# A fused attention, routing and feed-forward kernel: its pieces up to run 1 in a new sequence, the weights behind run 1's rows, half the rope table, the values' high parts on ScalarE

## The chip, the cores and the metric

One core of one Trainium2 chip runs the whole program. The metric is the device time of one execution in microseconds (us). The kernel before takes 654.41 us, the median of 3 runs (654.29 to 654.86).

## The reference

Three layers, one behind the other, all in float32:

```
q_rot, k_rot = rotate(q), rotate(k)                 # rope; 2 batches, 8 heads, 576 tokens, head size 64
attn = softmax(q_rot @ k_rot.T / 8)                 # per head
x = (attn @ v), heads side by side                  # 1152 tokens x 512
logits = x @ w_gate + log1p(exp(x @ w_noise)) * noise    # 8 experts
top2 experts per token, weights by softmax over the two
out[t] = sum over its two experts e: weight * relu(x[t] @ w1[e]) @ w2[e]      # 512 -> 1024 -> 512
h = out @ w_in;  g = max(h, 0) + log1p(exp(-|h|));  result = g @ w_out        # 512 -> 2048 -> 512
```

## The kernel before, in words

Matmuls of full precision are done as three products of a high and a low part (`mm3`). A value x is split by a copy into the shorter matmul format (the high part, on ScalarE) and a subtraction x - high (the low part, mostly on VectorE).

**Attention.** The 16 heads are worked on in 8 pairs. For each pair SyncE loads q, k and v (`load_pair`, `load_v`), GpSimd applies the rope in pieces (`ro`, `rope`) and splits the values into high and low parts in two passes (`vsplit`, L404 and L405). TensorE transposes q and k (`prep`), ScalarE and VectorE take high and low parts (`ph`, `pl`). Then two DMAs per pair rearrange them inside SBUF: `dq` (`move_queries`, L450) moves the queries to the other half of the partitions, and `dk` (`keys_twice`, L454) copies the keys into the half that the queries left, so `dk` can only be issued when `dq` has landed. Only then can the scores of the pair begin. The scores come in 72 blocks of 128 query rows, 9 per pair: S0 to S8 are pair 0, S9 is the first of pair 1, S13 the first of pair 1 that needs both heads, S36 the first of pair 4, S63 the first of pair 7. Each block n goes through S (TensorE, L479), M (row maximum, VectorE, L492), E (exponential, ScalarE, L501), T (transposes, TensorE, L510), Th and Tl (high and low parts, ScalarE L542 and VectorE L546), A (times the values, TensorE), Ao (copy, ScalarE), X (times the gate weights, TensorE L579), Xd (VectorE, which also issues the store of the rows to the table `xtab` from SyncE, L610 and L612).

**Routing.** The gate logits are added up (`l`). The first four token tiles are routed early (`R`), the others after the last head (`m`), with the ranking of the experts (`k`). That gives the row numbers of run 0 (`ga0` gathers them) and of run 1 (`ga1`, L1019, two indirect DMAs issued by GpSimd).

**Expert runs.** Runs 0 to 8 each take one expert's rows through w1, relu, w2. Run 0's first product (`G`) stands at the end of the planned part. Runs 0 and 1 use the same expert, whose 8 weight chunks of 512 KB are loaded (`ld`, `load_chunk`, L155) and split (`sp` on ScalarE L184, `sl` on VectorE or GpSimd L188) in the planned part. Chunks 8 onwards are loaded by SyncE, four ahead, as soon as the order of the experts is known. The feed-forward layer's weights are decoded and split in between.

**What sets the order.** Everything up to the end of run 0's first product is a list of about 900 pieces, the text `ORDER`, which was worked out offline from a table of pieces with an engine, a cost in ns and predecessors (the calls of `op`). The kernel emits the pieces in this order, so that each engine's queue and SyncE's DMA queue hold their pieces in the order of the list. An engine does not step past an instruction that waits, nor does SyncE's queue.

Of the kernel before, what the change touches and what calls it, by code (L numbers as in the profile page):

```python
# [50 lines left out]
ORDER = """
c0 rf-1 in0 rf0 rf4 rf1 kd0 prep0,2,0 rf5 in1 ph0,2,0 prep0,0,1 pl0,2,0 ph0,0,1 rf2 prep0,0,0 pl0,0,1 ph0,0,0 ro1,0
pl0,0,0 prep0,2,1 ph0,2,1 ro1,1 pl0,2,1 rf3 S0 ro1,2 S1 ro1,3 M0 kd1 lp2 M1 prep0,1,0 E0 ro1,4 prep0,1,1 ph0,1,0 S2
ro1,5 E1 pl0,1,0 ro1,6 ph0,1,1 M2 prep1,2 T0,1 ph1,2 ro1,7 pl0,1,1 S3 E2 pl1,2 ro1,8 prep1,0 Th0,1 M3 S4 ro1,9 ph1,0
Tl0,1 E3 ro1,10 pl1,0 T0,2 T0,0 rope1 M4 Th0,2 dq1,0 S5 Th0,0 vs0 Tl0,2 prep1,1 E4 M5 T0,3 S6 Tl0,0 Th0,3 dk1,0 E5 M6
T0,4 Th0,4 Tl0,3 rs0 S7 T0,5 E6 ro2,0 Tl0,4 Th0,5 lv2 S8 M7 ph1,1 T1,1 ro2,1 M8 A0,0 lp3 E7 Tl0,5 Th1,1 pl1,1 S9 E8
ro2,2 T1,2 Tl1,1 Ao0,0 A0,1 dq1,1 M9 Th1,2 ro2,3 ri0 E9 Tl1,2 T1,0 S10 Ao0,1 Th1,0 T1,4 ro2,4 dk1,1 M10 X0 Th1,4 Tl1,0
E10 S11 Tl1,4 rope2 T1,3 M11 S12 Th1,3 T2,1 Xd0 rs1 E11 lp4 prep2,0 vs1 M12 A1,0 ph2,0 ri1 Tl1,3 Th2,1 pl2,0 S13 Ao1,0
Tl2,1 E12 prep2,2 prep2,1 M13 ph2,2 lv3 T2,0 ph2,1 ro3,0 pl2,2 S14 Th2,0 pl2,1 A1,1 E13 M14 dq2 rs2 Tl2,0 T2,4 Ao1,1
S15 Th2,4 ro3,1 T2,5 M15 X1 E14 Tl2,4 dk2 Th2,5 ro3,2 Xd1 E15 T2,2 Tl2,5 S16 Th2,2 ro3,3 S17 Tl2,2 T2,3 M16 T3,0 Th2,3  # L60
A2,0 ro3,4 E16 Tl2,3 M17 Th3,0 T3,2 Ao2,0 rope3 Tl3,0 A2,1 Th3,2 ri2 E17 Tl3,2 S18 vs2 Ao2,1 prep3,2 T3,4 M18 ph3,2
S19 Th3,4 pl3,2 T3,3 M19 X2 E18 Tl3,4 E19 c1 S20 Xd2 Th3,3 T3,1 M20 S21 Th3,1 Tl3,3 prep3,1 E20 prep3,0 Tl3,1 ph3,1
T4,1 M21 rs3 S22 ph3,0 c3 ro4,0 lv4 pl3,1 E21 pl3,0 T4,0 Th4,1 A3,0 M22 Th4,0 dq3 l1 ro4,1 Tl4,1 E22 S23 Tl4,0 T4,3
M23 S24 ro4,2 Th4,3 T4,2 E23 Tl4,3 dk3 A3,1 Th4,2 l2 M24 rs4 Ao3,0 Tl4,2 T4,4 Ao3,1 S25 ro4,3 Th4,4 X3 M25 E24 Tl4,4
T4,5 ro4,4 E25 lp5 S26 c2 T5,1 ri3 Th4,5 M26 A4,0 Th5,1 rope4 Tl4,5 E26 Xd3 S27 Ao4,0 ri4 rs5 Tl5,1 T5,4 lp6 S28 vs3
Th5,4 ri5 prep4,0 M27 A4,1 ph4,0 M28 E27 Tl5,4 T5,2 Ao4,1 S29 pl4,0 Th5,2 T5,0 E28 M29 X4 Th5,0 Tl5,2 E29 prep4,1 Xd4
S30 ph4,1 Tl5,0 prep4,2 T6,2 ph4,2 ro5,0 pl4,1 S31 Th6,2 pl4,2 M30 dq4 T5,3 M31 l3 A5,0 E30 ro5,1 Tl6,2 Th5,3 S32 E31
Tl5,3 ro5,2 T6,3 Ao5,0 M32 dk4 S33 Th6,3 T6,1 E32 M33 ro5,3 A5,1 Th6,1 Tl6,3 E33 Tl6,1 S34 Ao5,1 ro5,4 T6,0 M34 T6,4
Th6,0 S35 Th6,4 Tl6,0 X5 rope5 M35 E34 T7,1 Tl6,4 E35 rs6 S36 lp7 prep5,2 Th7,1 Xd5 T7,0 l4 ph5,2 Tl7,1 vs4 prep5,0
S37 pl5,2 ph5,0 M36 T6,5 Th7,0 A6,0 M37 E36 pl5,0 Th6,5 S38 l5 Tl7,0 E37 prep5,1 Tl6,5 T7,4 Ao6,0 ro6,0 S39 M38 Th7,4  # L70
T7,2 M39 A6,1 E38 Tl7,4 ro6,1 Th7,2 S40 ph5,1 Tl7,2 E39 pl5,1 ro6,2 T7,3 M40 T8,1 dq5 Th7,3 S41 ri6 Ao6,1 rs7 Tl7,3
A7,0 Th8,1 ro6,3 E40 Tl8,1 T8,2 ri7 M41 T8,0 rs8 Th8,2 dk5 A7,1 Th8,0 Tl8,2 ro6,4 E41 Tl8,0 S42 Ao7,1 T8,4 Ao7,0 M42
S43 rope6 Th8,4 T8,5 ri8 M43 X6 E42 lv6 Tl8,4 E43 S44 Xd6 lv5 Th8,5 prep6,0 M44 X7 ph6,0 Tl8,5 E44 pl6,0 S45 rs9 Xd7
T9,4 T9,1 Th9,4 M45 z1 S46 vs5 ri9 prep6,2 Th9,1 A8,0 Tl9,4 ph6,2 E45 Tl9,1 T8,3 M46 S47 Th8,3 pl6,2 T9,0 E46 M47
prep6,1 Th9,0 Tl8,3 S48 ro7,0 E47 Tl9,0 T9,3 ph6,1 M48 S49 Th9,3 l6 pl6,1 E48 l7 T9,2 Tl9,3 dq6 R0 S50 M49 Ao8,0 R1
T10,2 Th9,2 M50 A8,1 E49 Tl9,2 ro7,1 E50 R2 S51 dk6 Th10,2 S52 ro7,2 Ao8,1 A9,0 M52 R3 T10,0 Tl10,2 Ao9,0 A9,1 Th10,0
ro7,3 M51 Tl10,0 lv7 E51 RP4 T10,5 RF4 T10,4 Ao9,1 ro7,4 S53 Th10,5 X8 Th10,4 Tl10,5 rope7 M53 E52 T10,1 X9 Tl10,4 E53
R6 Th10,1 Xd8 T11,4 S54 Xd9 Th11,4 z2 R7 prep7,2 Tl10,1 S55 ph7,2 prep7,1 Tl11,4 T10,3 ph7,1 pl7,2 cr0 T11,0 Th10,3
M54 A10,0 Th11,0 pl7,1 E54 Tl10,3 prep7,0 Ao10,0 Tl11,0 S56 R8 ph7,0 ld0 T11,2 M55 T11,3 Th11,2 M56 A10,1 Th11,3 ld3
Tl11,2 E55 Tl11,3 R9 T11,1 E56 pl7,0 S57 Th11,1 T12,1 dq7 Ao10,1 S58 Tl11,1 Th12,1 M57 sp0 rs10 T12,2 Tl12,1 A11,0  # L80
Th12,2 l9 M58 E57 vs6 dk7 Tl12,2 T12,0 E58 S59 ri10 Th12,0 T12,3 M59 S60 Ao11,0 Th12,3 Tl12,0 A11,1 E59 M60 sl0 Tl12,3
T12,4 E60 z0 S61 T13,0 Th12,4 M61 S62 rs11 X10 E61 Tl12,4 rs12 Ao11,1 M62 S63 R10 Th13,0 T13,1 E62 M63 A12,0 ld1
Tl13,0 Th13,1 E63 Tl13,1 S64 ld2 Ao12,0 ri11 T13,4 Xd10 T12,5 Th13,4 M64 S65 l10 Th12,5 X11 z3 Tl13,4 rs13 E64 vs7
Tl12,5 T13,3 sp1 M65 S66 T14,0 Th13,3 Xd11 A12,1 E65 ri12 Tl13,3 M66 S67 z4 Th14,0 E66 Tl14,0 T13,2 Ao12,1 M67 RP11
T14,3 Th13,2 RF11 S68 E67 Tl13,2 A13,0 Th14,3 M68 rs14 sp2 Tl14,3 T14,2 ld4 l11 sl1 S69 ga0 Th14,2 T14,1 E68 A13,1
Tl14,2 Ao13,0 Th14,1 M69 T14,4 Ao13,1 S70 Tl14,1 Th14,4 gl0 X12 M70 E69 Tl14,4 T14,5 E70 S71 Xd12 T15,0 Th14,5 M71 l12
X13 Th15,0 ri13 Tl14,5 E71 A14,0 Tl15,0 sp3 Xd13 T15,1 sl2 l13 Ao14,0 T15,4 rs15 Th15,1 A14,1 Th15,4 Tl15,1 ld6 XT1
Tl15,4 Ao14,1 T15,3 XTh1 XT0 XTl1 ld5 T15,2 ri14 XTh0 A15,0 Th15,3 XTl0 Th15,2 Tl15,3 X14 Ao15,0 Tl15,2 sp4 sl3 A15,1
Xd14 ld7 Ao15,1 ri15 l14 sl4 sp5 X15 G0 Xl15 l15 Xd15 m0 G1 m1 Gh0 Gl0 G2 m2 Gh1 m3 Gh2 mP4 Gl2 G3 mF4 Gl1 m6 G4 k0
Gh3 m7 Gl3 G5 Gh4 k1 Gl4 m8 G6 Gh5 k2 sp6 m9 G7 Gh6 sl5 Gl5 mP10 mF10 Gh7 Gl6 ga1 sl6 sp7 k3 sl7 k4 Gl7 k5  # L90
# [1605 lines left out]
```

## Time and profile before

| | |
|---|---|
| time, median of 3 | 654.41 us |
| time of the profiled execution | 653.66 us |
| its span in the profile | 651.8 us |
| TensorE busy | 626.5 us (96%) |
| VectorE busy | 481.3 us (74%) |
| ScalarE busy | 420.3 us (64%) |
| GpSimd busy | 223.4 us (34%) |
| DMA traffic | 109.79 MB |

The page slices the span into 40 equal parts; TensorE's line of tenths there reads 9 nearly everywhere, and the clock line reads 9 except in the first slice. A busy TensorE is not one at its peak, because the ends of its matmuls are modelled; an engine's waits stand in brackets behind its rows in a timeline. The attention ends near 174 us, run 0's first product near 187 us, run 1 begins near 202 us and the feed-forward layer near 437 us.

### The profile page before, as it was taken

Reading aid. Unit: us, or ns where it says so; the run is one execution under the profiler, and the core shown is the slowest. Engines: PE = TensorE matmul, PEld = TensorE weight load, DVE = VectorE, ACT = ScalarE, POOL = GpSimd, SP = SyncE. Lnnn points to the kernel's source line nnn. Section 1 sums busy time; section 2 is a strip of 40 time slices with the busy share of each in tenths; the row PEclk is TensorE's granted clock in tenths of the full one; section 3 lists DMA queues with packets and bytes.
Section 4 is the critical chain, followed back from the end, with each engine's and each line's share of the span. In section 5 each row is a group of like instructions: output and inputs, shape, how many; then the busy total and the mean of one; then the engine's idle time right before and its main releaser. Section 6 shows DMA issues by size and latency. Waiting matters only on the chain.

```text
span 651.8 us, 11560 instructions
## 1 busy us (share of the span) xinstructions
PE 626.5 (96%) x3944; PEld 561.3 (86%) x3944; DVE 481.3 (74%) x979; ACT 420.3 (64%) x883; POOL 223.4 (34%) x318
## 2 busy tenths in 40 slices
...
GB/s 142 118 158 109 168 119 192 167 216 272 114 112 241 220 226 332 311 274 349 303 333 292 342 312 304 278 205 167 126 33 33 33 17 1 48 2 2 33 1 33
DMA packets 70061, 109.79 MB, mean 168 GB/s; under 512 B 11728, under 2 KB 39120, under 8 KB 69616
## 3 DMA queue, kind: packets, MB, share of 16 engines
...
q10 hardware_dynamic: 3426, 5.79, 2.4%
...
HBM read 76.70 MB, written 23.59 MB: 154 GB/s over the span
## 4 chain that ended last, share of the span: by engine, by line
PE 75%; DMA 9%; DVE 6%; issue 4%; ACT 3%; POOL 2%; SPq 0%; DVEq 0%; POOLq 0%; ACTq 0%
PE p L264 9%; PE p L266 9%; PE p L265 9%; PE po L266 5%; PE ph L264 5%; PE ph L265 5%; PE ph L266 5%; PE po L264 5%; PE po L265 5%; PE ps L479 4%; DMA wb<-wb 3%; PE pt L510 3%; PE pa L557 2%; PE p L1282 2%; DMA qT<-wb 1%
## 5 line engine op out<-in xcount | busy, mean ns | idle before, releaser
L233 POOL TENSOR_TENSOR dm<-dm,da 128x512 int32<-128x512 int32 x32 | 41.9, 1310 | 134.4 <-DVE da L230 78.3
L1574 ACT ACTIVATE fa<-ph 128x256 f32<-128x256 f32 (+1 forms) x64 | 26.0, 407 | 69.2 <-PE ph L266 69.2
L492 DVE TENSOR_REDUCE nmx<-ps 128x1 f32<-128x576 f32 x72 | 53.5, 749 | 11.6 <-PE ps L479 11.2
L1264 DVE SCALAR_TENSOR_TENSOR hb<-p,hb 128x256 fp32r<-128x256 f32 (+1 forms) x104 | 31.8, 345 | 33.0 <-ACT hb L1262 32.9
L501 ACT ACTIVATE P<-ps,nmx 128x576 f32<-128x576 f32 x72 | 53.4, 745 | 4.2 <-DVE nmx L492 2.8
L188 DVE TENSOR_TENSOR w<-wraw,w 128x1024 fp32r<-128x1024 f32 x41 | 55.2, 1354 | 0.5 <-ACT w L184 0.5
L1581 DVE TENSOR_SCALAR fu<-fa 128x256 f32<-128x256 f32 (+1 forms) x64 | 19.8, 310 | 46.9 <-ACT fa L1575 46.8
...
L546 DVE TENSOR_TENSOR ptl<-pt,pth 128x512 fp32r<-128x512 f32 x72 | 48.3, 682 | 3.1 <-ACT pth L542 2.4
L542 ACT ACTIVATE pth<-pt 128x512 fp32r<-128x512 f32 x72 | 42.7, 601 | 10.1 <-PE pt L510 9.7
L184 ACT ACTIVATE w<-wraw 128x1024 fp32r<-128x1024 f32 x42 | 44.1, 1055 | 7.1 <-DMA wraw<-in_moe_w_dram 5.6
L264 PE MATMUL p<-xh,w 128*128 128x256 f32 (+3 forms) x152 | 46.5, 306 | 0.0
L265 PE MATMUL p<-xl,w 128*128 128x256 f32 (+3 forms) x152 | 46.5, 306 | 0.0
L266 PE MATMUL p<-xh,w 128*128 128x256 f32 (+3 forms) x152 | 46.5, 306 | 0.0
L188 DVE TENSOR_TENSOR wb<-wraw,wb 128x1024 fp32r<-128x1024 f32 x33 | 45.1, 1374 | 0.2 <-ACT wb L184 0.2
L510 PE MATMUL pt<-ident,P 128*128 128x128 f32 x288 | 43.7, 278 | 1.1 <-DVE ptl L546 0.5
L510 PEld LDWEIGHTS pt<-ident,P 128*128 128x128 f32 x288 | 34.2, 142 | 2.8 <-DVE ptl L546 1.1
L1582 DVE TENSOR_TENSOR fa<-fa,fu 128x256 f32<-128x256 f32 (+1 forms) x64 | 29.4, 460 | 9.6 <-ACT fl L1576 7.4
L184 ACT ACTIVATE wb<-wraw 128x1024 fp32r<-128x1024 f32 x33 | 34.6, 1054 | 0.3 <-DMA wraw<-in_moe_w_dram 0.2
L1262 ACT ACTIVATE hb<-p 128x320 fp32r<-128x320 f32 (+3 forms) x64 | 26.1, 420 | 13.3 <-PE p L266 12.2
L479 PE MATMUL ps<-wb,qT 128*128 128x288 f32 (+1 forms) x160 | 29.6, 314 | 4.8 <-DMA wb<-wb 3.5
L1593 ACT ACTIVATE gh<-fl 128x256 fp32r<-128x256 f32 (+1 forms) x64 | 27.7, 432 | 9.4 <-DVE fl L1587 9.4
...
## 6 DMA issues: line engine op xcount, KB each, us to landing
...
```

The lines of the kernel that those rows point to most:

```text
L184: nc.scalar.activation(hi, r, AF.Copy)
L188: lo_eng.tensor_tensor(out=lo, in0=r, in1=hi.bitcast(F32), op=OP.subtract)
L233: nc.gpsimd.tensor_tensor(out=m, in0=m, in1=ai, op=OP.add)
L264: nc.tensor.matmul(ps, ah, bh, start=first and i == 0, stop=False)
L265: nc.tensor.matmul(ps, ah, bl, start=False, stop=False)
L266: nc.tensor.matmul(ps, al, bh, start=False, stop=last and i == n - 1)
L479: nc.tensor.matmul(ps[:m, a, :HN], QT[p][:, c0:c0 + m], KK[p][:, x, hh, k0:k0 + HN], start=x == 0, stop=x == 1)
L492: nc.vector.tensor_reduce(out=nmx, in_=stS[n][:, :, :HN], axis=AX.XY, op=OP.max, negate=True)
L501: nc.scalar.activation(P_of(n).rearrange("p (a c) -> p a c", a=2), ps[:, :, :HN], AF.Exp, bias=nmx, scale=1.0, accum_out=acc)
L510: nc.tensor.transpose(ps[:, kb, :], Pt[:, kb * 128:(kb + 1) * 128], ident)
L542: nc.scalar.activation(dh, x, AF.Copy)
L546: nc.vector.tensor_tensor(out=dl, in0=x, in1=dh.bitcast(F32), op=OP.subtract)
```

## The change

- `ORDER` is a new list, worked out again from new costs. SyncE's costs are larger (loads of q and k 2150 to 2700 ns, of v 1100 to 2900), some others smaller.
- The store of a head pair's rows is a piece of its own (`xo`) and no longer a part of `Xd`. The loads of the gate weights are a piece of their own (`gt`) and no longer behind `lp2`.
- The high parts of the values move from GpSimd to ScalarE (`vh`); the low parts stay on GpSimd (`vs`).
- The rope table has 5 blocks for each partition instead of 9. It is loaded by SyncE behind the first keys; the other four are copied by ScalarE.
- A DMA of 64 bytes, `seen`, reads run 1's second tile of rows. It stands on SyncE's queue ahead of the loads of chunks 8 to 11.
- The ranking of the experts moves from GpSimd to VectorE except for its last part; 4 of the 10 one-hot rows of the late routing move from VectorE to GpSimd (`oa`).
- The loads of chunks 4 to 7 become pieces of the list (`ld4` to `ld7`); before, the low part of the chunk four earlier issued them.

```diff
 ORDER = """
-c0 rf-1 in0 rf0 rf4 rf1 kd0 prep0,2,0 rf5 in1 ph0,2,0 prep0,0,1 pl0,2,0 ph0,0,1 rf2 prep0,0,0 pl0,0,1 ph0,0,0 ro1,0
+c0 rf-1 in0 rf0 rf4 rf1 kd0 prep0,2,0 rf5 prep0,0,0 ph0,2,0 rf2 ph0,0,0 pl0,2,0 pl0,0,0 prep0,2,1 ph0,2,1 rf3
...
-    def load_pair(p, heads=((0, 2),), queues=(nc.sync, nc.sync)):
+    def load_pair(p, heads=((0, 2),), queues=(nc.sync, nc.sync), then=None):
...
+                if then and i:
+                    then()
...
-    def vsplit(p, eng):
...
-        eng.tensor_tensor(out=tt[:, :, 0:D], in0=xx, in1=zb, op=OP.add)
-        eng.tensor_tensor(out=tt[:, :, D:2 * D], in0=xx, in1=tt[:, :, 0:D].bitcast(F32), op=OP.subtract)
+    def v_hi(p):
+        x, t = v_parts(p)
+        nc.scalar.activation(t[:, :, 0:D], x, AF.Copy)
+
+    def v_lo(p):
+        x, t = v_parts(p)
+        nc.gpsimd.tensor_tensor(out=t[:, :, D:2 * D], in0=x, in1=t[:, :, 0:D].bitcast(F32), op=OP.subtract)
...
+    def X_store(g):
+        b, h = divmod(g, H)
         if h % 2:
...
     def ranks():
...
-        fold(g, above, rank)
-        yield
+        V.tensor_tensor(out=above, in0=kc[:, None, :].to_broadcast(sq), in1=kc[:, :, None].to_broadcast(sq), op=OP.is_lt)
+        V.tensor_reduce(out=rank, in_=above, axis=AX.X, op=OP.add)
...
-        g.tensor_tensor(out=srt[:, 0], in0=ohR, in1=kc[:, None, :].to_broadcast(sq), op=OP.mult)
-        g.tensor_tensor(out=srt[:, 1], in0=ohR, in1=iota8[:, None, :].to_broadcast(sq), op=OP.mult)
-        fold(g, srt, srt[:, :, :, 2])
...
+        V.tensor_tensor(out=srt[:, 0], in0=ohR, in1=kc[:, None, :].to_broadcast(sq), op=OP.mult)
+        V.tensor_tensor(out=srt[:, 1], in0=ohR, in1=iota8[:, None, :].to_broadcast(sq), op=OP.mult)
+        V.tensor_reduce(out=srt2, in_=srt, axis=AX.X, op=OP.add)
...
-    nc.scalar.dma_start(out=cs[:, 0:5], in_=cs_t[:, 0:5])
-    load_pair(0, ((0, 1),), (nc.scalar, nc.sync))
+    load_pair(0, ((0, 1),), (nc.scalar, nc.sync), lambda: nc.sync.dma_start(out=cs[:, 0:5], in_=cs_t))
     nc.scalar.activation(csq[:, 0:5], cs[:, 0:5], AF.Copy, scale=0.125)
-    nc.sync.dma_start(out=cs[:, 5:9], in_=cs_t[:, 5:9])
-    nc.scalar.activation(csq[:, 5:9], cs[:, 5:9], AF.Copy, scale=0.125)
+    nc.scalar.activation(cs[:, 5:9], cs[:, 0:4], AF.Copy)
+    nc.scalar.activation(csq[:, 5:9], cs[:, 0:4], AF.Copy, scale=0.125)
...
-        op(("vs", p), "POOL", 2850, [("A", 2 * p - x, a) for x in (4, 3) for a in (0, 1)] + [("lv", p)] if p > 1 else [("in", 1)], vs_op, p)
+        op(("vh", p), "ACT", 610, [("A", 2 * p - x, a) for x in (4, 3) for a in (0, 1)] + [("lv", p)] if p > 1 else [("in", 1)], v_hi, p)
+        op(("vs", p), "POOL", 1600, [("vh", p)], v_lo, p)
         if p > 1:
-            op(("lv", p), "SP", 1100, [("vs", p - 2)], load_v, p)
+            op(("lv", p), "SP", 2900, [("vs", p - 2)], load_v, p)
         if p > 2:
-            op(("lp", p), "SP", 2150, [("rope", p - 2)], load_pair, p)
+            op(("lp", p), "SP", 2700, [("rope", p - 2)], load_pair, p)
...
-    op(("lp", 2), "SP", 2150, [("rf", 3), ("rf", 5)], lambda: (load_pair(2), load_gates()))
+    op(("lp", 2), "SP", 2700, [("rf", 3), ("rf", 5)], load_pair, 2)
+    op(("gt", 0), "SP", 5600, [], load_gates)
...
+    op(("oa", 0), "DVE", 1440, [("m", 6)], one_hots, nc.vector, 0, 6)
+    op(("oa", 1), "POOL", 2360, [("m", 6)], one_hots, nc.gpsimd, 6, 10)
...
     nxt["order"] = True
+    nc.sync.dma_start(out=seen, in_=XG[1, 1][0:1, 0:16])
     while nxt["load"] < nxt["split"] + 4:
         load_chunk()
...
-    tok = np.stack(four + [512 + p % 64] + four, axis=1)
+    tok = np.stack(four + [512 + p % 64], axis=1)
```

SyncE's queue before, from the first copies of pair 1 (`qT`, `wb`: L450 is `dq`, L454 is `dk`) to the second ones; L366 and L369 load values, L358 and L361 load k and q:

```order
L450 DMA qT_302<-wb_78 64x640 x2
L454 DMA wb_78<-wb_78 64x2x640
L366 DMA w3_140<-in_v_dram 128x2x256
L369 DMA w3_140<-in_v_dram 64x2x64 x2
L358 DMA w3_140<-in_k_dram 128x2x256
L361 DMA w3_140<-in_k_dram 128x1x64
L358 DMA w3_140<-in_q_dram 128x2x256
L361 DMA w3_140<-in_q_dram 128x1x64
L450 DMA qT_302<-wb_78 64x512 x2
L454 DMA wb_78<-wb_78 64x2x640
```

The same place now (L461 is `dq`, L465 is `dk`, L363 and L368 load k and q):

```order
L461 DMA qT_301<-wb_79 64x640 x2
L465 DMA wb_79<-wb_79 64x2x640
L461 DMA qT_301<-wb_79 64x512 x2
L363 DMA w3_141<-in_k_dram 128x2x256
L368 DMA w3_141<-in_k_dram 128x1x64
L363 DMA w3_141<-in_q_dram 128x2x256
L368 DMA w3_141<-in_q_dram 128x1x64
L465 DMA wb_79<-wb_79 64x2x640
```

The second head's queries are no longer queued behind seven loads, and the load of values has left this stretch; the load of k and q stands between the second pair of copies.

SyncE's queue before at the copies of pair 7, with two weight chunks (L155, which need the expert's number from L130):

```order
L1004 DMA ytab_62<-wb_78 128x4x512
L130 TENSOR_LOAD ordA_91
L130 ISA x2
L155 ISA
L155 DMA wraw_1925<-in_moe_w1_dram 128x4x256
L155 ISA
L155 DMA wraw_1963<-in_moe_w1_dram 128x4x256
L450 DMA qT_1852<-wb_78 64x1152 x2
L454 DMA wb_78<-wb_78 64x2560
```

The same place now:

```order
L1016 DMA ytab_62<-wb_79 128x4x512
L461 DMA qT_1834<-wb_79 64x1152 x2
L134 TENSOR_LOAD ordA_92
L134 ISA x2
L159 ISA
L159 DMA wraw_2040<-in_moe_w1_dram 128x4x256
L465 DMA wb_79<-wb_79 64x2560
```

The queries' move now stands ahead of the expert's number and of any weight chunk; one chunk instead of none lies between the move and the keys' copy.

SyncE's queue before at the end of the planned part, from the last chunk of run 0's expert:

```order
L155 DMA wraw_2508<-in_moe_w2_dram 128x2x512
L610 DMA xtab_60<-xs_2520 128x4x128
L612 DMA xtab_60<-xs_2520 64x128
L130 TENSOR_LOAD ordr_92
L130 ISA x2
L155 ISA
L155 DMA wraw_2786<-in_moe_w1_dram 128x4x256
```

The same place now:

```order
L624 DMA xtab_60<-xs_2524 128x4x128
L626 DMA xtab_60<-xs_2524 64x128
L159 ISA
L159 DMA wraw_2573<-in_moe_w2_dram 128x2x512
L1312 DMA seen_63<-yg_2436 1x16
L134 TENSOR_LOAD ordr_93
L134 ISA x2
L159 ISA
L159 DMA wraw_2785<-in_moe_w1_dram 128x4x256
```

The small read of run 1's rows (`seen`) stands ahead of the load of the experts' order and of chunk 8.

## Rows read from the trace of the kernel before

**Rows 1.** PE's timeline: start us, us, operation, count, idle before and releaser.

```profile
30.88 0.37 PE L479 MATMUL ps<-wb,qT 128*128 128x288 f32 x1 [1.36 <-ACT o L568]
...
40.44 1.29 PE L479 MATMUL ps<-wb,qT 128*128 128x288 f32 x8 [0.93 <-DMA wb<-wb]
...
87.03 0.76 PE L479 MATMUL ps<-wb,yg 128*128 128x288 f32 x4 [0.84 <-DMA wb<-wb]
...
144.67 0.77 PE L479 MATMUL ps<-wb,qT 128*128 128x288 f32 x4 [2.54 <-DMA wb<-wb]
...
174.11 1.35 PE L579 MATMUL pa<-Wx,o 128*128 128x96 f32 x10 [0.56 <-ACT o L568]
...
195.11 0.63 PE L1246 MATMUL pa<-ident,yg 128*128 128x128 f32 x4 [0.78 <-DMA yg<-xtab,idx]
...
199.70 0.84 PE L1246 MATMUL pa<-ident,yg 128*128 128x128 f32 x4 [2.57 <-DMA yg<-xtab,idx]
```

**Rows 2.** Stretches: us, busy of PE, PEld, DVE, ACT, POOL, clock, DMA share, GB/s.

```profile
60.00:140.00 80.00, 78.48 (x626) 75.97 (x625) 74.88 (x147) 70.02 (x178) 65.13 (x104) 1.00 0.63 161
140.00:160.00 20.00, 17.46 (x137) 17.31 (x136) 15.35 (x28) 15.09 (x37) 11.29 (x23) 0.91 0.90 271
...
200.00:205.00 5.00, 5.00 (x28) 4.40 (x27) 1.66 (x3) 1.90 (x4) 2.95 (x3) 0.66 0.57 181
...
240.00:400.00 160.00, 160.00 (x914) 138.30 (x913) 120.35 (x199) 103.59 (x169) 50.43 (x42) 1.00 0.92 315
```

**Rows 3.** Chain that ended last, the copies of pairs 4 and 7: start, us, what.

```profile
77.58 3.93 DMA yg<-wb
81.57 5.33 DMA wb<-wb
...
132.72 5.79 DMA qT<-wb
138.56 5.97 DMA wb<-wb
```

**Rows 4.** SP's timeline, the loads ahead of pair 7's copies.

```profile
129.94 0.99 SPq L155 DMA_DIRECT2D wraw<-in_moe_w_dram  x2
131.04 2.15 SPq L450 DMA_DIRECT2D qT<-wb  x2
```

**Rows 5.** Timeline of DVE and SP, pair 1's last low part and its move.

```profile
29.32 0.68 DVE L442 TENSOR_TENSOR wb<-pa,wb 128x512 fp32r<-128x512 f32 x1
...
32.19 1.29 SPq L450 DMA_DIRECT2D qT<-wb  x2
```

**Rows 6.** Timeline of POOL and SP around the gather of run 1's rows.

```profile
187.71 0.79 POOL L1067 TENSOR_TENSOR wb<-csq,wb 128x128 fp32r<-128x128 f32 x2
188.59 2.87 SPq L155 DMA_DIRECT2D wraw<-in_moe_w_dram  x4
188.64 1.85 POOL L1019 DMA_INDIRECT yg<-xtab,idx  x1 [0.15 <-issue]
190.80 1.09 POOL L1019 DMA_INDIRECT yg<-xtab,idx  x1 [0.30 <-issue]
```

**Rows 7.** DMA issues, 186 to 192.5 and 200 to 206: last number us to landing.

```profile
yg<-xtab,idx POOLq DMA_INDIRECT x2, 7.6
...
xg<-xtab,idxr POOLq DMA_INDIRECT x3, 3.7
```

**Rows 8.** DMA queues from 194 to 196: packets, MB, share.

```profile
q1 hardware_dynamic: 564, 0.56, 91.7%
q0 software_dynamic: 25, 0.06, 8.2%
```

**Rows 9.** Groups of the page: ScalarE's copies of 512 and 1024 columns.

```profile
L542 ACT ACTIVATE pth<-pt 128x512 fp32r<-128x512 f32 x72 | 42.7, 601 | 10.1 <-PE pt L510 9.7
L184 ACT ACTIVATE w<-wraw 128x1024 fp32r<-128x1024 f32 x42 | 44.1, 1055 | 7.1 <-DMA wraw<-in_moe_w_dram 5.6
```

**Rows 10.** ACT's timeline, the first and the fifth split in run 1.

```profile
204.57 1.05 ACT L184 ACTIVATE wb<-wraw 128x1024 fp32r<-128x1024 f32 x1
...
211.54 1.06 ACT L184 ACTIVATE w<-wraw 128x1024 fp32r<-128x1024 f32 x1 [1.19 <-DMA wraw<-in_moe_w_dram]
```

**Rows 11.** DVE's timeline, the first row maxima.

```profile
14.79 1.42 DVE L492 TENSOR_REDUCE nmx<-ps 128x1 f32<-128x576 f32 x2
```

More of the change, by code (lines that the diff above doesn't have):

```diff
@@ L56 @@
[L56 to L60, printed above, removed]
@@ L116, in fused_kernel @@
     ytab = dram.tile([NROW * 128, DM], F32, name="ytab")
+    seen = dram.tile([1, 16], F32, name="seen")
     consts = ctx.enter_context(tc.tile_pool(name="consts", bufs=1))
@@ L182, in split_hi, with second @@
         r = chunk_raw.pop(s)
-        lo_eng = nc.gpsimd if s < 1 else nc.vector
+        lo_eng = nc.gpsimd if s in LOW_POOL else nc.vector
         nc.scalar.activation(hi, r, AF.Copy)
         chunk[s] = (hi, lo)
-        def second():
+        def second(load=True):
             lo_eng.tensor_tensor(out=lo, in0=r, in1=hi.bitcast(F32), op=OP.subtract)
-            load_chunk()
+            if load:
+                load_chunk()
         lo_q.append(second)
@@ L782, in fused_kernel, with one_hots @@
     rko = rko.rearrange("p (t x) b -> p t x b", x=2)
+    srt2 = rr.tile([128, 2, E], F32, name="srt2")
     rix = tmpq([(E - 1) * CB, E]).rearrange("p (r t) e -> p r t e", t=CB)
+    one_hot = {}
+    def one_hots(eng, i0, i1):
+        ohA, pmf = one_hot["A"]
+        for i in range(i0, i1):
+            eng.tensor_scalar(ohA[:, i, :], iotaA, pmf[:, i // 2, i % 2:i % 2 + 1], None, op0=OP.is_equal)
     def route():
@@ L1178, in fused_kernel @@
     op(("cr", 0), "POOL", 2300, [("R", 7)], choose_rest)
-    op(("ga", 0), "POOL", 2500, [last[0], ("S", 62), ("vs", 7), ("rope", 7), ("Xd", 9), ("rs", 14)], gather_A)
+    op(("ga", 0), "POOL", 3400, [last[0], ("S", 62), ("vs", 7), ("rope", 7), ("xo", 7), ("rs", 14)], gather_A)
     op(("gl", 0), "SP", 4200, [("ga", 0)], lambda: None)
```

161 lines of the change are left out of this document (76 added, 85 removed).

## The prediction

> **What bounds the kernel now.** I read the stretches first, then TensorE's waits in its timeline, then the chain that ended last around each of those waits, and last the queues that the chain named there. The stretches [rows 2] show three different regimes. From 60 to 140 us TensorE, VectorE and ScalarE are all nearly full: 78.48, 74.88 and 70.02 of 80 us. No single engine sets the pace there; a wait on one can be absorbed by another's arrears. From 240 to 400 TensorE is busy for all of the 160 us and shows no wait, at the full clock. So what is won or lost before run 1 passes through to the end one for one, as long as the weights keep up. Between them lie places where TensorE simply stands still. Its timeline [rows 1] names seven: scores of pair 1 (1.36 and 0.93), of pair 4 (0.84), of pair 7 (2.54), the last head's product (0.56), and the two tiles of run 1's rows (0.78 and 2.57). Two of them are followed by a granted clock below full speed: 0.91 over 140 to 160, and 0.66 over 200 to 205 [rows 2]. [...]
>
> For the waits inside attention, what ends last are the two DMAs per pair, the queries' move and behind it the keys' copy. In pair 4 they take 3.93 and 5.33 us, in pair 7 5.79 and 5.97 [rows 3]. For run 1 it is the gather of its rows: issued at 188.64 and 190.80, with four weight loads issued at 188.59 on SyncE [rows 6], and landed after a median of 7.6 us; the next gathers, when the loads are through, land after 3.7 [rows 7].
>
> **The change part by part.** The sum is made against the profiled execution, 653.66 us; the median of the runs is 654.41, so 0.75 is added at the end.
>
> *Run 1's rows.* `seen` cannot be issued before the second tile has landed, so SyncE holds chunks 8 to 11 until then. With 3.7 us instead of 7.6, the second tile, issued at 190.80, lands at 194.5. TensorE asks for it at 199.70 - 2.57 = 197.1. So the 2.57 goes, and with it the slow clock behind it: 2.57 + 1.7 = 4.3 us. I leave the 0.78 before the first tile in place, since TensorE also has a branch there. Bounds: nothing, if the gather takes 199.70 - 190.80 = 8.9 as before, and 5.1 if the 0.78 goes too.
>
> What is queued behind `seen` are the loads of chunks 8 to 11 and, behind them, SyncE's part of the branch. They begin about 6 us later than 188.59. ScalarE wants chunk 8 for its first split at 204.57 [rows 10], which now comes 4.3 earlier, at 200.3. An issue at 195.5, 512 KB at 315 GB/s [rows 2] or 1.6 us, and some 2 us of latency (3.7 less the 0.8 of a tile of 256 KB, less issue time) give 199.1. That is just in time; the fifth split waited 1.19 us before [rows 10] without a wait of TensorE. I take nothing, with bounds of 0 and 2: a split that waits blocks the relu behind it on ScalarE, and TensorE would feel it only through its four output buffers.
>
> *Pair 7.* The second half of the move goes out at 132.72 [rows 3], but the queue has taken two chunks of 512 KB at 129.94, ahead of it [rows 4]. The two copies then take 11.8 us against 9.3 in pair 4 [rows 3]. Now the move goes ahead of every chunk and one chunk lies before the keys' copy: 3.9 + 1.6 + 5.3 = 10.8, one less. One more piece of TensorE's stands between the last low part and S63 (16 instead of 15, by the lists), worth some 0.2; the 15 last from 132.72 to 144.67 - 2.54 = 142.13, 0.63 us apiece. The wait falls from 2.54 to about 1.3. A wait of 0.84 left the clock at 1.00 [rows 1, 2], 2.54 did not; I take 1.3 to be harmless. Gain 1.2 + 1.8 = 3.0; bounds 0 and 4.3.
>
> *Pair 1.* The second head's last low part ends at 30.00, the move is issued at 32.19 behind seven loads [rows 5]. Now it stands directly behind the first head's keys, and the low part itself comes far earlier: 22 pieces of TensorE's before S13 instead of 13. The 0.93 goes; bounds 0 and 0.93, since a load of k and q now stands between its two copies. The first head's S9 has one transposing piece more before it, and the gate weights' eight issues are out of the way of its move. Of its 1.36 I take 0.6; bounds 0 and 1.36.
>
> *Pair 4.* Its 0.84 lies where VectorE is 94% busy [rows 2]; what comes late next is VectorE's own queue, so I count nothing; bounds 0 and 0.84.
>
> *Last head.* The last copies of head 15 (`Ao15,1`) now have head 14's gate product in front of TensorE's wait: 0.5 of the 0.56.
>
> *Values' high parts.* A copy of 640 columns on ScalarE is not in the trace. Between 601 ns for 512 columns and 1055 for 1024 [rows 9] it is 601 + 454 x 128/512 = 715 ns, 5.7 us for eight. Most fall where ScalarE has 10 free us in 80 [rows 2]; they stand in order in its queue ahead of exponentials and high parts. Bounds: a loss of 5.7, and nothing. GpSimd loses eight passes, but nobody on the chain waits for it, so no gain. I take a loss of 1.0, nearer to the idle time that is there.
>
> *Start.* The keys' small last block now queues behind the rope table on SyncE, the queries no longer do on ScalarE's queue. VectorE does the second head's rope before the first scores instead of after them, and TensorE one transposing piece more. The first row maxima had been held to 14.79 [rows 11] by exactly that rope; I see them at 14 to 15.5. Nothing, bounds 1 either way.
>
> *Ranking and one-hot rows.* The index matmul stands behind run 0's last product in both lists, so what moves between VectorE and GpSimd there is covered by that product; if the cover is gone, up to 1.0 is lost. Nothing.
>
> Sum: 4.3 + 3.0 + 0.9 + 0.6 + 0.5 - 1.0 = 8.3. 653.66 - 8.3 = 645.4, and with 0.75, 646.1.
>
> **The rivals.** *Attention gives nothing.* A new sequence of 900 pieces opens as many small holes as it closes, because in the full stretch 60 to 140 every engine is at 88 to 98%. For it: those shares. Against: the waits of pairs 1 and 7 lie outside that stretch. Only the rows' 4.3 remain: 654.4 - 4.3 = 650.1.
>
> *The weights are not what holds the rows.* Then `seen` returns little. In the trace the gathers' queue had 8.2% of the DMA engines from 194 to 196 and the weights' queue 91.7% [rows 8], while both had work. [...]
>
> *The loads between the two copies make more pairs wait (slower).* The new queue sets the load of k and q (640 KB) between move and keys' copy of pairs 2 and 3, and a chunk in pair 7. Pair 7 shows the price of 1 MB ahead: 11.8 - 9.3 = 2.5 us, and 1.8 of clock. If pairs 2 and 3 pay 4.3 each and pair 7's gain of 3.0 is lost, 646.1 + 11.6 = 657.7. It decides once both wait over 2.5 us. Against it: between last low part and first scores the lists hold 18 pieces of TensorE's instead of 13 in pair 2, 21 instead of 14 in pair 3, 17 instead of 13 in pair 4. For it: the move and copy of pair 2 need at least 9.3 plus 2.0 of load, and 18 pieces at 0.63 last 11.3.
>
> *The weights' stream is the bound (slower).* The DMA engines are 92% busy from 240 to 400 [rows 2]; a stream that begins 6 later, less attention's 4.0, would end 2 later: 656.4. Against it: TensorE has no wait in these 160 us, and from 200 to 205 the engines are only 57% busy, so the stream has room to catch up.
>
> **How the numbers follow.** The forecast 646.1 has a chance of 0.50, attention without gain 0.20, rows without gain 0.10, the wedged loads 0.15, the stream 0.05. The forecast's own terms reach from 640.5 (all waits gone) to 651. For 8 in 10 I take 640 to 656, which leaves out part of the two slower cases. 0.2% of the time, 1.3 us, is about what a measurement can tell from no change. The first three cases lie beyond it but for their edges: faster 0.77, same 0.06, slower 0.17.
>
> **What would show it.** Right: no wait over 1 us before the second tile of run 1's rows, the gather landing within 5 us, a clock of 1.00 in the 5 us behind it; S63's wait under 1.6 us and a clock of 1.00 after it; S13 without a wait; run 0's last product ending near 183 instead of 187; TensorE without a wait from run 1 to run 8. Wrong: a gather that still takes 7 us with nothing else in flight; waits of 2 us at the first scores of pairs 2 or 3; ScalarE's splits in run 1 waiting so long that TensorE does; VectorE filling the freed time so that run 0's product ends where it did.

## The result, and the profile after

The changed kernel takes 647.87 us (median of 5 runs, 646.09 to 648.65), the kernel before 654.41 in the same comparison (5 runs, 652.59 to 659.64). The ratio of their mean times is 0.9887, with a 95% interval of 0.9843 to 0.9932. The forecast was 646.1. The profiled execution took 647.63 us with a span of 645.8, 6.0 less than before.

Six places show how the lead came about, from the first row maximum to the first rows of the feed-forward layer; the last line is the end of the span.

| | before, us | after, us | lead |
|---|---|---|---|
| first row maximum | 14.79 [rows 11] | 16.91 | -2.1 |
| TensorE begins run 0's first product | 175.25 | 169.48 | 5.8 |
| TensorE begins run 0's second product | 187.23 | 182.50 | 4.7 |
| TensorE takes the second tile of run 1's rows | 199.70 [rows 1] | 191.89 | 7.8 |
| TensorE takes the last run's first tile | 387.40 | 378.35 | 9.0 |
| TensorE takes the feed-forward layer's first rows | 433.38 | 427.15 | 6.2 |
| end of the span | 651.8 | 645.8 | 6.0 |

So 9.0 us were won by the last run, with the 2.1 lost at the start already taken off, and 2.8 were given back between there and the feed-forward layer. TensorE's timeline after (start, us, operation, count, idle before and releaser): S18, S63, the index matmuls between run 0's two products, the two tiles of run 1's rows, and the feed-forward layer's first rows.

```profile
51.18 0.77 PE L490 MATMUL ps<-wb,yg 128*128 128x288 f32 x4 [1.15 <-DMA w<-in_v_dram]
...
141.26 0.76 PE L490 MATMUL ps<-wb,qT 128*128 128x288 f32 x4
...
181.88 0.19 PE L875 MATMUL pa<-P 128*128 128x30 f16 x1 [0.32 <-POOL P L803]
182.46 0.19 PE L875 MATMUL pa<-P 128*128 128x30 f16 x1 [0.39 <-POOL P L803]
...
190.03 0.63 PE L1254 MATMUL pa<-ident,yg 128*128 128x128 f32 x4 [0.45 <-PEq L1440]
191.89 0.60 PE L1254 MATMUL pa<-ident,yg 128*128 128x128 f32 x4
...
427.15 1.12 PE L1520 MATMUL pa<-ident,yg 128*128 128x128 f32 x4 [4.27 <-DVE yg L1514]
```

Of the seven waits in [rows 1] none is left: S63 and the second tile follow without one, and before the first tile there is only the branch's 0.45. The largest new one inside attention stands at S18. Its row names a load of values, which stands on SyncE's queue behind the keys' copy of pair 2; that it is this copy which S18 waits for is shown by an experiment below.

Two small new waits stand at the index matmuls, and they are where the lead falls from 5.8 to 4.7. They wait for the four one-hot rows that moved to GpSimd, for which the list had 2360 ns; the timeline of GpSimd shows 3.64 us:

```profile
178.77 3.64 POOL L803 TENSOR_SCALAR P<-iotaA,P 128x128 f16<-128x128 f16 x4
```

Before, the ten index matmuls followed each other within 0.41 us, without a wait. The last row of the timeline above has its counterpart before in

```profile
433.38 0.66 PE L1511 MATMUL pa<-ident,yg 128*128 128x128 f32 x4 [1.74 <-DVE yg L1505]
```

where the wait is 1.74. The stretches after that answer to [rows 2], and two around the feed-forward layer's start (columns as there, the clock after the five engines):

```profile
140.00:160.00 20.00, 19.86 (x162) 19.30 (x161) 18.37 (x34) 18.96 (x46) 8.13 (x12) 1.00 0.73 237
200.00:205.00 5.00, 5.00 (x46) 5.00 (x45) 3.83 (x5) 1.53 (x3) 0.95 (x1) 1.00 1.05 406
240.00:400.00 160.00, 160.00 (x920) 140.21 (x920) 117.14 (x199) 105.19 (x171) 50.96 (x42) 1.00 0.90 313
420.00:430.00 10.00, 5.73 (x22) 4.44 (x21) 2.95 (x4) 1.66 (x2) 3.22 (x3) 0.76 0.69 251
430.00:440.00 10.00, 8.81 (x59) 7.62 (x59) 4.47 (x10) 6.13 (x13) 3.41 (x4) 0.90 0.47 153
```

The clock is 1.00 where it had been 0.91 and 0.66, and TensorE is still never idle from 240 to 400. The slow clock has moved to 420 to 440.

The gather of run 1's rows, which answers to [rows 6] and [rows 7]: the timeline of GpSimd's issues, of the read `seen` and the first loads on SyncE, and of the cast on VectorE that makes the experts' order known.

```profile
183.27 1.93 POOL L1031 DMA_INDIRECT yg<-xtab,idx  x1 [0.16 <-DVE dl L878]
185.51 1.37 POOL L1031 DMA_INDIRECT yg<-xtab,idx  x1 [0.31 <-issue]
...
189.42 0.31 SPq L1312 DMA_DIRECT2D seen<-yg  x1
191.00 1.02 SPq L159 DMA_DIRECT2D wraw<-in_moe_w_dram  x2
...
187.57 0.16 DVE L676 CAST ordr<-srt 128x8 int32<-128x8 f32 x1
```

The DMA issues from 182 to 187 (the last number is the median time to landing):

```profile
yg<-xtab,idx POOLq DMA_INDIRECT x2, 3.9
```

It lands after 3.9 us, as forecast (3.7). But the order, without which no load can go, is known only at 187.7, 2.2 us behind the gather's second issue; before, the loads left 2.2 us ahead of that issue [rows 6]. So two things keep the loads away here, and only one of them was in the prediction. The collision has moved on to the next gather: it is issued at 192.97 among the four loads and lands after 6.9 us instead of 3.7 [rows 7], without a wait of TensorE.

What is given back begins on GpSimd (timeline; its last decoding step before the gather of the feed-forward layer's rows, then the gather), goes on to ScalarE, which stands in order behind that gather, and so to the store of the last run's first tile:

```profile
403.17 1.29 POOL L238 TENSOR_TENSOR dm<-dm,da 128x512 int32<-128x512 int32 x1 [6.84 <-ACT dm L227]
408.81 1.77 POOL L1501 DMA_INDIRECT yg<-ytab,yrow  x1 [4.34 <-issue]
...
412.97 0.72 ACT L1510 ACTIVATE yg<-yg,wts 128x512 f32<-128x512 f32 x1 [3.06 <-DMA yg<-ytab,yrow]
415.65 0.59 ACT L1297 ACTIVATE y<-p 128x512 f32<-128x512 f32 x1
416.28 0.36 ACTq L1304 DMA_DIRECT2D ytab<-y  x1
```

The semaphores that the gather waits for had their last update before it at 402.9, before its predecessor had even begun, hence "issue" as the releaser. The DMA queues from 404 to 409 (packets, MB, share) show one packet of another kind, begun at 406.89:

```profile
q14 instruction: 1, 0.01, 0.4%
```

Before, the same gather follows its predecessor at once:

```profile
411.80 1.30 POOL L233 TENSOR_TENSOR dm<-dm,da 128x512 int32<-128x512 int32 x1 [6.29 <-ACT dm L222]
413.25 0.97 POOL L1492 DMA_INDIRECT yg<-ytab,yrow  x1
```

### The profile page after: what moved, and what is told of

The parts are those of the page before. It is cut to its first block, busy times and chain, and to the rows that moved or that the text cites. A ratio compares the mean times of both kernels' runs of the same rounds, so it can differ in the third digit from the quotient of the medians.

```text
span 645.8 us, 11559 instructions
## 1 busy us (share of the span) xinstructions
PE 622.5 (96%) x3944; PEld 556.7 (86%) x3944; DVE 480.4 (74%) x981; ACT 423.4 (66%) x892; POOL 214.1 (33%) x304
## 4 chain that ended last, share of the span: by engine, by line
PE 63%; issue 2%; DVE 2%; DMA 1%; ACT 1%; POOL 1%; ACTq 0%; DVEq 0%; POOLq 0%
PE p L269 10%; PE p L270 10%; PE p L271 10%; PE po L271 5%; PE po L270 5%; PE po L269 5%; PE ph L269 5%; PE ph L270 5%; PE ph L271 5%; PE p L1290 2%; PE pa L1254 1%; PE p L1292 1%; DMA yg<-ytab,yrow 1%; POOL yg L1501 1%; PE px L1520 0%
## 5 line engine op out<-in xcount | busy, mean ns | idle before, releaser
L192 DVE TENSOR_TENSOR w<-wraw,w 128x1024 fp32r<-128x1024 f32 x41 | 53.9, 1322 | 5.1 <-ACT w L188 5.1
L1501 POOL DMA_INDIRECT yg<-ytab,yrow x18 | 21.4, 1189 | 92.3 <-PE px L1520 68.2
L521 PE MATMUL pt<-ident,P 128*128 128x128 f32 x288 | 42.3, 274 | 0.9 <-DVE ptl L557 0.6
L490 PE MATMUL ps<-wb,yg 128*128 128x288 f32 (+1 forms) x160 | 30.6, 320 | 2.3 <-ACT P L512 1.2
```

Of the source, the lines that this page charges most:

```text
L521: nc.tensor.transpose(ps[:, kb, :], Pt[:, kb * 128:(kb + 1) * 128], ident)
```

## The experiments

The runs were made on other chips than the first comparison, where the kernel before had medians of 652.4 to 653.6 and single runs from 648.7 to 657.0. So I go by ratios to it (with their 95% intervals in brackets), by kernels timed side by side, and by the traces. A trace is read for its waits, and the time from the medians.

### The read taken out of the changed kernel

```diff
-    nc.sync.dma_start(out=seen, in_=XG[1, 1][0:1, 0:16])
```

> The changed kernel without the 64-byte read of run 1's rows; nothing else is altered. Theory A (the read is what frees the gather, the prediction's step): the loads of chunks 8 to 11 go out while the gather is in flight, its tiles land after 6 us or more, TensorE waits 1.5 to 3 us for the second tile, the clock behind it falls, and the time is 3 to 4.5 us more than the 647.9 of the changed kernel: 651 to 652.5. Rival B (the ranking, which now stands behind the gather on GpSimd and ends on VectorE near 187.7, already keeps the loads back until the gather is nearly through): the gather lands in 4 to 5 us, TensorE waits under 0.7 us, the loads go out near 188.2 instead of 191.0, and the time is 647 to 648.5, no worse than with the read.

Measured: 647.1 us, 0.9917 (0.9894 to 0.9940). The gather lands after 4.3, the loads leave at 190.31, TensorE has no wait at the second tile. Theory A fell, and rival B holds: in the changed kernel the read is worth nothing that shows, because the order of the experts is known so late that the loads stay away without it.

### The read put into the kernel before

```diff
     nxt["order"] = True
+    nc.sync.dma_start(out=seen, in_=XG[1, 1][0:1, 0:16])
```

> The kernel before with the 64-byte read of run 1's second tile put ahead of the loads of chunks 8 to 11, nothing else altered. There the gather is issued at 188.6 and 190.8 and the loads at 188.6. Theory A and B alike (loads in flight slow the gather): its tiles land in 4 us, the wait of 2.57 us goes and the clock behind it stays at 1.00; 4.3 less, 650.1. [...] Given-back variant D: run 1 begins 4 us earlier, but the waits near 430 grow and only 1 to 2.5 us are left: 652 to 653.5.

Measured: 651.58 us, 0.9978 (0.9956 to 0.9999): 1.4 less by the ratio, 1.1 by the medians, just clear of nothing. The gather's time to landing, from the DMA issues:

```profile
yg<-xtab,idx POOLq DMA_INDIRECT x2, 4.5
```

The timeline of SyncE and TensorE, the first loads and the one wait in run 1:

```profile
198.38 1.42 SPq L156 DMA_DIRECT2D wraw<-in_moe_w_dram  x2
...
216.14 0.51 PE L265 MATMUL p<-wb,hb 128*128 128x512 f32 x1 [0.64 <-ACT hb L1263]
```

And who waited for the loads of the chunks, from 195 to 225 (us, times):

```profile
  ACT w L185: 4.2, 3
  ACT wb L185: 2.3, 2
```

With the loads held back, the gather lands after 4.5 us instead of 7.6 [rows 7], and the 2.57 us wait is gone: loads in flight do slow it. But in run 1 ScalarE's splits now wait 6.5 us for the weights (3.7 before) and TensorE comes up 0.8 short between 210 and 220. Its lead over the kernel before falls from 1.6 us at the second tile to 1.0 at the last tile of the last run, though the slow clock at 200 is gone. Variant D had the size nearly right (652 to 653.5) and the place wrong: it is given back in run 1, not at 430.

### The ranking ahead of the gather again, without the read

```diff
-... G4 mF4 m6 G5 ... ga1 sp7 k0 sl7 Gl6 Gl7 k1 k2 k3
+... G4 mF4 k0 k1 m6 G5 ... ga1 sp7 sl7 Gl6 Gl7 k2 k3
-    nc.sync.dma_start(out=seen, in_=XG[1, 1][0:1, 0:16])
```

> The changed kernel without the 64-byte read and with the first two parts of the ranking (the experts' order) put ahead of the one-hot rows on VectorE, so that the order is known some 8 us before the gather of run 1's rows instead of 2 us after its second issue. Theory A (loads in flight slow the gather; in the changed kernel it is the late ranking that keeps them away, and the read adds nothing to it): the loads of chunks 8 to 11 go out from 178 on, the gather's tiles land after 5.5 to 8 us instead of 3.9 to 4.3, and TensorE waits 1 us or more for the second tile; 649 to 651, of which up to 1.8 us comes from VectorE's chain being that much longer. Rival B (loads do not slow it): tiles land in 4 to 4.5 us, no wait above 0.6 us at the rows, time 647 to 649.

Measured: 648.8 us, 0.9927 (0.9890 to 0.9964). The gather's time to landing:

```profile
yg<-xtab,idx POOLq DMA_INDIRECT x2, 5.4
```

The timeline, SyncE's loads and TensorE's tiles:

```profile
180.26 7.32 SPq L159 DMA_DIRECT2D wraw<-in_moe_w_dram  x4
...
193.00 0.63 PE L1254 MATMUL pa<-ident,yg 128*128 128x128 f32 x4 [0.45 <-PEq L1439]
194.86 0.60 PE L1254 MATMUL pa<-ident,yg 128*128 128x128 f32 x4
```

The landing is 1.5 us slower, just under A's range, but no wait comes of it: these loads leave one by one over 7 us, and TensorE asks for the second tile 7.9 us behind its issue. Between the theories: slowed, and hidden. TensorE now waits elsewhere, 0.49 and 1.13 us at the index matmuls, for VectorE and GpSimd, and the clock from 180 to 190 is 0.83. Three of the four loads left ahead of the gather's second issue, so no run has the changed kernel with four loads leaving together with the gather.

### The old queues for the first loads

```diff
-    load_pair(0, ((0, 1),), (nc.scalar, nc.sync), lambda: nc.sync.dma_start(out=cs[:, 0:5], in_=cs_t))
+    nc.scalar.dma_start(out=cs[:, 0:5], in_=cs_t)
+    load_pair(0, ((0, 1),), (nc.scalar, nc.sync))
```

> The changed kernel with the first loads on the queues of before: the (half) rope table first on ScalarE's queue, the queries behind it, and the keys' last block directly behind the keys on SyncE. Theory A (the table wedged between the two loads of the keys costs the 2.1 us by which the first row maximum is now late, 16.9 against 14.8, and this passes through): first maximum at 15 to 15.5, 1.4 to 2 us less, 646 to 646.5. Rival B (a late start is taken up by the waits of pair 1 and 2, since the lead at S18 is already 1.8 us): first maximum earlier, S18 waits longer, time 647.5 to 648.3. Rival C (queries behind the table delay GpSimd's rope as much): first maximum stays at 16.5 or later, same time.

Measured: 647.88 us, 0.9919 (0.9891 to 0.9947). The first row maximum comes at 15.45, but S18 now waits 2.03 us instead of 1.15, and the last row maximum is at 157.0 against 156.3. Rival B in the time: the earlier start is lost again at S18, part of it to the longer wait for pair 2's copy, and the rest to the clock, which behind that wait is 0.83 from 50 to 60. The ten profiles with the new queues have the first maximum between 15.85 and 17.34, so 15.45 in one profile makes the queues a likely cause of the late start; which of the two queues it is was not told apart.

### The values' high parts on GpSimd again

```diff
-        nc.scalar.activation(t[:, :, 0:D], x, AF.Copy)
+        nc.gpsimd.tensor_tensor(out=t[:, :, 0:D], in0=x, in1=zb, op=OP.add)
```

> The changed kernel with the values' high parts back on GpSimd (a pass of 128x640 each, 8 in all), at the same places of the list. Theory A (on ScalarE the eight copies cost about 1.0 us, the prediction's term): 646.9 or so, and ScalarE's busy time 5.9 us less. Rival B (ScalarE hides them, and GpSimd's passes of some 1.3 us in front of the low parts and the rope make it late): waits of TensorE on values or rope pieces, 648.5 to 650. Rival C (neither is on the path): 647.5 to 648.3.

Measured: 647.86 us, 0.9940 (0.9917 to 0.9963). From the first to the last row maximum it takes 139.5 us, the changed kernel 139.4. Rival C, as far as these runs can tell: on neither engine do they show on the path.

### Two weight chunks ahead of pair 7's move

```diff
-... T11,3 dq7 Ao10,1 ... Tl12,0 ld0 T12,3 ... S62 ld3
+... T11,3 ld0 ld3 dq7 Ao10,1 ... Tl12,0 T12,3 ... S62
```

> The changed kernel with its first two weight chunks put ahead of the queries' move of pair 7, as they stood before; nothing else moved. Theory A (the prediction's: 1 MB ahead of the move and its copy is what made S63 wait 2.54 us): the move and the copy take 11 to 12 us together, S63 waits 1.5 to 3 us, the clock of the 20 us behind it falls below 1.00, and the time is 2 to 4 us more: 650 to 652. Rival B (the new list has so many pieces between the last low part and S63 that it hides the copies with the chunks ahead too): S63 waits under 0.5 us, 647.3 to 648.5.

Measured: 650.62 us, 0.9973 (0.9946 to 0.9999); beside it, on the same chip, the next kernel 647.26. S63 in TensorE's timeline:

```profile
143.93 1.30 PE L490 MATMUL ps<-wb,qT 128*128 128x288 f32 x4 [2.90 <-DMA wb<-wb]
```

and the stretch around it, with its clock:

```profile
140.00:160.00 20.00, 17.10 (x127) 16.93 (x125) 14.24 (x26) 15.19 (x38) 6.73 (x10) 0.91 0.80 219
```

Theory A: the wait of 2.54 and the clock of 0.91 [rows 1, 2] are back with the chunks, at a price of 2.7 against the changed kernel's median and 3.4 against the kernel beside it. From the move's second half (130.81) to S63 it takes 13.1 us, somewhat more than the 11 to 12 expected.

### Pair 4's loads behind pair 2's copy

```diff
-... dq2 ... T2,2 lp4 M13 ... Ao1,1 dk2 M15
+... dq2 ... T2,2 M13 ... Ao1,1 dk2 lp4 M15
```

> The changed kernel with the loads of pair 4's keys and queries behind the keys' copy of pair 2 instead of between its move and its copy. Theory A (the loads wedged in between make the copy land 8.0 us after its issue, at 51.09, and S18 waits 1.15 us for it): the copy takes 5 to 6 us, S18 does not wait, and the time falls by 0.5 to 1.2: 646.7 to 647.4. Rival B (the loads of values and noise behind the copy slow it as much): S18 waits 0.8 us or more as before, same time. Rival C (what S18 gains, VectorE takes back within pair 3): no wait at S18, the row maxima from S27 on as late as before, 647.5 to 648.3.

Measured: 647.26 us, 0.9934 (0.9908 to 0.9960). No wait at S18 any more, but one at S27, where pair 5's loads lie in the same way between move and copy:

```profile
68.58 0.78 PE L490 MATMUL ps<-wb,qT 128*128 128x288 f32 x4 [1.12 <-DMA wb<-wb]
```

From the first to the last row maximum 138.6 us instead of 139.4. The mechanism is shown: this is the copy that S18 waited for. The 0.8 us are too little for these medians.

### 14 more instructions on GpSimd, ahead of the gather and behind it

```diff
     for r in range(1, NR):
+        for _ in range(14 * (r == 4)):
+            nc.gpsimd.memset(rank1[:, 0:1], 0.0)
```

> The changed kernel with 14 one-column memsets more on GpSimd at the start of run 4, where it is idle; all else as it is. In the changed kernel GpSimd stands idle for 4.3 us before the first gather of the feed-forward layer's rows (408.81) with every semaphore it waits for already there, and a packet of 8 KB of kind instruction is seen 1.6 us before it goes on; in the kernel before, whose list on GpSimd is 14 instructions longer up to that place, neither is there (0.15 us). Theory A (GpSimd waits for its own program to be fetched, at a place set by the number of instructions ahead): with 14 more the gather follows its predecessor within 0.5 us, TensorE's wait before the first rows falls from 4.27 to 1.5 to 2.5, and the time by 1.5 to 3: 645 to 646.5. Rival B (the wait has to do with what VectorE or the DMA queues do at that time): 4 to 4.6 us again before the gather, 647.5 to 648.5. Rival C (the idle time is there but not on the path): gather earlier, TensorE's wait still near 4, 647.5 to 648.3.

Measured: 643.91 us, 0.9887 (0.9854 to 0.9919), 3.4 less than the kernel of the section above beside it. (Its ratio is the same as that of the changed kernel in the first comparison, where the kernel before ran slower; the kernel timed beside it is the one to go by.) GpSimd at the gather, then TensorE:

```profile
403.42 1.29 POOL L238 TENSOR_TENSOR dm<-dm,da 128x512 int32<-128x512 int32 x1 [6.52 <-ACT dm L227]
404.87 0.97 POOL L1501 DMA_INDIRECT yg<-ytab,yrow  x1
...
425.13 0.66 PE L1520 MATMUL pa<-ident,yg 128*128 128x128 f32 x4 [1.67 <-DVE yg L1514]
```

The 4.34 is gone, TensorE's wait is 1.67, and the clock from 420 to 440 is 1.00. No packet of kind instruction is near the gather any more (none from 400 to 406); one lies at 364.6 instead. The control, with the same memsets behind the gather:

> A control: the 14 memsets stand behind the gathers of the feed-forward rows instead of ahead of them (they fall into the wait for the last run's rows). If the number of instructions ahead of the gather decides (theory A), GpSimd stands idle for 4.2 to 4.6 us before the first of these gathers as in the changed kernel, with a packet of kind instruction 1.6 us before it goes on, and TensorE waits about 4 us. If 14 more instructions anywhere in the program do it (rival), the gather follows within 0.5 us.

Measured, a single time: 648.27 us; a packet of kind instruction at 407.45, and

```profile
403.54 1.29 POOL L238 TENSOR_TENSOR dm<-dm,da 128x512 int32<-128x512 int32 x1 [5.96 <-ACT dm L227]
409.37 1.57 POOL L1501 DMA_INDIRECT yg<-ytab,yrow  x1 [4.54 <-issue]
```

So what counts here is the number of instructions ahead of the gather: 14 more ahead of it take the 4.34 us away, 14 behind it leave 4.54. An attempt to bring the wait about in the kernel before put 115 memsets more on GpSimd, 23 at the start of each of runs 2 to 6, so that the same gather stands 129 instructions further on than in the changed kernel:

> [...]

Measured: 653.05 us, 1.0009 (0.9981 to 1.0038); 0.15 us before the gather, 1.20 us of TensorE's. A packet came at 412.27, while the third gather was being issued (412.06 to 413.00), and delayed nothing that shows. The attempt failed, and what sets the place stays open.

### Both repairs together

The 14 memsets, and the loads of pairs 4 and 5 behind the copies of pairs 2 and 3.

> The changed kernel with the 14 GpSimd memsets in run 4, and with the loads of keys and queries of pairs 4 and 5 behind the keys' copies of pairs 2 and 3 instead of between move and copy. If both effects stand by themselves: no wait at S18 and S27, 0.8 to 1.5 us less in attention, the wait before the feed-forward rows 1.2 to 2.5 us, 642.5 to 643.5. Rival (attention gives nothing: VectorE takes it back): as with the memsets alone, 643.5 to 644.5.

Measured: 642.06 us (641.46 to 642.72), 0.9821 (0.9787 to 0.9855): each of the six runs lies below each of the changed kernel's five. No wait at S18 or S27; 137.9 us from the first to the last row maximum, and 1.96 before the feed-forward rows. The time is 0.4 below the range set for both effects together.

### The last run's loads behind its first store as well

```diff
-            (1, 2): [lambda: ygather(1, 1), let_loads], ...
+            (1, 2): [lambda: ygather(1, 1), put_seen, let_loads], ...
+    def put_seen():
+        nc.sync.dma_start(out=seen, in_=ytab[r0:r0 + 1, 0:16])     # r0: the last run's first row
```

> The kernel of the run before last (14 memsets, loads behind copies), and in the last run a 64-byte read of the rows that its first tile has stored, ahead of the five weight loads that are held back there: SyncE lets them go only when that store has landed. Theory A (loads in flight slow that store, 4.7 to 6.3 us, and the gather behind it, 3.3 to 5 us, as they did the gather of run 1's rows): the store lands in 3 to 4 us, TensorE's wait before the feed-forward rows falls below 0.5 us, and the time by 1.2 to 2.5: 640.5 to 642. Rival B (store and gather take that long by themselves): the wait stays at 1.2 to 2.5 us, time 642.5 to 644. Rival C (slower): the five loads come 5 us later and ScalarE's splits of them hold up the first feed-forward blocks, waits of TensorE behind 435 of 1 us or more, 643.5 to 646.

Measured: 649.94 us, 0.9950 (0.9921 to 0.9978): 8 slower than without. The gather that the store releases, without and then with the read; the loads; TensorE:

```profile
419.17 0.97 POOL L1501 DMA_INDIRECT yg<-ytab,yrow  x1 [11.34 <-DMA ytab<-y]
```

```profile
414.47 0.97 POOL L1501 DMA_INDIRECT yg<-ytab,yrow  x1 [7.11 <-DMA ytab<-y]
414.92 9.17 SPq L159 DMA_DIRECT2D wraw<-wtab  x5
...
431.84 1.11 PE L1520 MATMUL pa<-ident,yg 128*128 128x128 f32 x4 [7.25 <-DVE yg L1514]
```

The store, issued at 412.3 and 412.2, is through 4.6 us sooner with no load in flight. But then four of the five loads leave within 2 us, on top of that gather (7.1 us to landing instead of 3.3) and of the second store, and TensorE waits 7.25 us for the second rows. Theory A for the store; the time is slower, as in C, but far outside its range, and by another mechanism than the one I had named.

## Why the prediction was right, and where it was not

*Pair 7* (3.0): right in the mechanism, and small in the size. S63 does not wait, the clock stays at 1.00, and putting the chunks back costs 2.7 to 3.4. The 1.3 of the wait that I left was not there. The 1.8 for the clock is an estimate, (1 - 0.91) x 20 us from [rows 2], like the 1.7 of run 1's rows, (1 - 0.66) x 5 us. No run shows either term apart from the wait ahead of it: the 2.7 to 3.4 are wait and clock together, and in the kernel before with the read, where the 2.57 us wait and the slow clock at 200 both went, 1.1 to 1.4 came of it. Nor is the clock slow in every execution: the profile of the kernel before with 115 memsets more, from 140 to 160 (columns as in [rows 2]), has S63 waiting 2.79 us and the clock at 1.00.

```profile
144.33 0.77 PE L479 MATMUL ps<-wb,qT 128*128 128x288 f32 x4 [2.79 <-DMA wb<-wb]
...
140.00:160.00 20.00, 17.21 (x147) 17.00 (x145) 16.25 (x30) 16.20 (x39) 11.92 (x22) 1.00 0.93 282
```

*Run 1's rows* (4.3): the wait and the slow clock went, and the gather landed as computed, but the step "SyncE holds chunks 8 to 11 until then" was not what did it: without the read the gather lands as well. I had set the ranking's move at nothing, and looked only at whether it delays the gather; I did not see that it delays the loads behind it. Either of the two alone is enough. The bound of 2 for late weights was rather small: in the kernel before, where the read makes the loads wait until 198.4, it gives 1.1 to 1.4 of the 4.3.

*The rival in which the weights do not hold the rows.* A tile's rows landed after 7.6 us among four loads issued together [rows 7], 5.4 among loads that left one by one, 4.5 without. If the company cost only one more transfer of the tile, 256 KB at 315 GB/s [rows 2] or an estimated 0.8 us, the rival would hold; the measured 3.1 decides against it, at this place.

*Pair 1 and the last head* (0.9, 0.6, 0.5): all three waits are gone, S9's whole 1.36 too. So is pair 4's 0.84, for which I counted nothing. The rival that expected no gain here rested on every engine being at 88 to 98% from 60 to 140; GpSimd was at 81% there (65.13 of 80 us [rows 2]).

*Start* (0, bounds 1): wrong in the row, 2.1 late; the new queues are the likely cause (15.45 with the old ones). In this kernel it cost nothing that shows in the time, since the wait for pair 2's copy and the clock behind it took back what the old queues won. With that wait mended it was not tried.

*Ranking and one-hot rows* (0, bound 1.0): wrong. The cover of run 0's product was not enough, and the lead falls by 1.0 us at the two waits for GpSimd. With the ranking ahead of the gather the waits there are longer (0.49 and 1.13 us).

*High parts* (-1.0): the copy takes 740 ns (715 computed), but the term is nothing that shows.

*The wedged loads*, the slower rival, were there at S18 with 1.15 us (up to 2.1 in other profiles with these loads), a quarter of the 4.3 set for a pair, and at S27 once S18 was mended. The lists' 18 pieces were indeed not quite long enough.

*What failed* is "what is won or lost before run 1 passes through to the end one for one". It did through run 8 (9.0 us), and then 2.8 were lost on a wait of GpSimd that none of my steps had. The seven waits that I read in TensorE's timeline left out those at the feed-forward layer's start (1.74 us at 433.38), so I had no eye on that place. With the wait removed, the same change gives 643.9.

*Luck.* That the sum came so near is in part errors that cancel. Attention and the start together were to give 4.0; they gave 5.8 by the start of run 0's first product, 7.9 without the late start, which is about all the waits of [rows 1] up to there with the clock's 1.8. Then 1.0 went at the one-hot rows. The rows of run 1 gave their 4.3, 2.8 went on GpSimd's wait, and 0.2 to 0.3 more by the end: 6.0 in the span instead of 8.3. And the 1.3 us that I called the limit of a measurement was too small, since the interval above is 2.9 us to either side.
